# Units 4 and 5 computed by halves of a chunk, and one visit of block 1 placed eight matmuls later

## The chip, the cores and the metric

The kernel runs on one core of a Trainium2 chip. The core has five engines with a queue of instructions each: PE (TensorE, matmuls, with PEld for its weight loads), DVE (VectorE), ACT (ScalarE), POOL (GpSimd) and SP (SyncE, which here only issues DMAs). The metric is the time of one execution on the device in microseconds (us).

## The reference

Two layers follow each other. The first is retention, a recurrence with a 64x64 state for each of 8 heads and 4 batches over 768 tokens. The second is a feed-forward network over all 3072 tokens with a parametric ReLU:

```python
for t in range(S):
    state = gamma * state + outer(k[:, :, t], v[:, :, t])
    y[:, :, t] = scale * (q[:, :, t] @ state)
x = y.transpose(0, 2, 1, 3).reshape(B * S, H * D)   # 3072 x 512
h = x @ w_in                                        # 512 x 2048
g = maximum(h, 0) + alpha * minimum(h, 0)
out = g @ w_out                                     # 2048 x 512
```

## The kernel before, in words

**Tiling.** Tokens are taken in 12 units of 256, three to a batch. A unit has two chunks of 128 tokens (`c` = 0, 1), and a chunk has two halves of 64 (`r` = 0, 1). The 8 heads are four pairs (`p`), with `a` the head within a pair. Two units are a block of 512 tokens; there are six blocks.

**Retention of a unit.** Instead of token by token it goes by chunks: products k·v summed over tokens (tiles `st`), a running state (`tf`, the state after the decay; `th`, its copies in 16 bits for the matmuls), scores k·q within the chunk (`sca`, `scb`), scores times a causal mask (`m`), and the output `y`, which is the state times q plus the masked scores times v. `y` is copied to `xT`, the input of the feed-forward network.

There are two forms of this in the kernel.

- *By chunks* (`sum_mm`, `state_sum`, `score_mm`, `masks`, `out_mm`): one state per chunk; the scores of the first half of the tokens run against all 128 queries of the chunk and those of the second half against 64.
- *By halves* (`halves_mm`, `middle`, `behind_middle`, `middle_copy`, `half_mm`, `half_masks`, `halves_out`): the sums stay apart for each half, a second state `tm` stands in the middle of the chunk, and scores are needed only within a half. `tm` is copied to 16 bits into one of six buffers `tgbuf`: the near half of the partitions by POOL, the far half by ACT (`part=1`). For each chunk, DVE makes `tm`, then `ss`; POOL multiplies `ss` by the decay and gives `tf`, from which DVE makes the next chunk's `tm`.

In the kernel before, units 4 and 5 go by chunks, and units 6 to 11 by halves (`MID = 6`).

**The loop around it.** The order of all work on every engine is written out by hand; no scheduler moves anything, and each engine takes its instructions in the order in which the code issues them. In pass `n` of the last loop (n = 1 to 4) the second layer of block n is computed and the retention of block n+1 is put between its matmuls. "Block 1" is the pass n = 1, with `u0` = 4 and `u1` = 5.

The second layer (`ffn2_seven`) is seven products of 16 matmuls each, called p1 to p7 below in their order, with a yield behind each matmul; `tick(gen, m)` issues m of them. They accumulate in two PSUM banks, `ox` (bank 0) and `oy` (bank 1):

- p1 writes `ox`; ACT copies `ox` to `oy` (`moves`).
- p2 adds to `ox`; ACT copies `ox` out as `os` (`kept`).
- p3 adds to `oy`; ACT copies `oy` out as `cu`.
- p4 begins `ox` anew.
- p5 adds to `oy`; ACT copies `oy` out as a second `cu`, which DVE adds to `ox` (`plus`).
- p6 adds to `oy` again; ACT copies it out as `ot`.
- p7 adds to `ox`; DVE adds the first `cu` and gives `os`.

A product that writes a bank waits until the copy out of that bank is done. In the code this stands as:

```python
        yield from product(oy, gs(1), ws(1), False)
        u2 = kept(oy)
        yield
        ox = bank(x, "ox")
        yield from product(ox, gs(0), ws(0), True)
        yield
        yield from product(oy, gs(2), ws(2), False)
        u3 = kept(oy)
        plus(ox, u3, "o1")
        yield
        yield from product(oy, gq(1, 1), ws(3), False)
```

**The visits.** Three times in a pass the retention's matmuls are put between those of the products. The *first visit*, behind p1 (`tick(gen, 16)`), has the sums of both units and the scores of `u0`. The *second*, in the middle of p4 (after ticks of 8, 9, 15 and 8), has the output of `u0` and the scores of `u1`. The *third*, behind p5 in all passes before (`tick(gen, 24)`), has the output of `u1`; four matmuls of the next block's first layer follow it (`begin(n + 1)`), then the rest of the products.

**Queries.** `move_q` copies the queries into a second arrangement `qf`. In block 1, ACT does it, in two instructions for each unit; for later units it is a DMA.

**Sums for p3 to p7.** `g_sums` are DVE additions over the whole activated tile. In block 1, DVE does the first two of them in one piece each, 2048 elements per partition, right before it turns to the retention; in later blocks they are in pieces of 1024, of which the first pieces come earlier.

Of the kernel before, what the change touches and what calls it, by code (L numbers as in the profile page):

```python
# [22 lines left out]
def kernel(  # L23
# [21 lines left out]


    SPLIT = 4
    MID = 6
    U = 256
    UPB = S // U  # L50
    NU = B * UPB
# [42 lines left out]
    HF, HM = NFT // 2, d_model // 2  # L94
# [16 lines left out]
    tgbuf = [tgall[:, i] for i in range(6)]  # L111
# [137 lines left out]
    def sum_mm(u, banks, half=0):  # L249

        kdq, _, vx = prepped[u]
        last = u % UPB == UPB - 1
        cs = (0,) if last else (0, 1)
        if half == 0:
            sums["t"] = [ps(banks[0], "st0"), ps(banks[1], "st1")]
        for p in range(NP):
            for r in range(2):
                for c in cs:
                    for a in range(2):
                        nc.tensor.matmul(  # L260
                            out=sums["t"][c][rows(a), 256 * half + 64 * p : 256 * half + 64 * p + 64],
                            lhsT=kdq[rows(c), 0, r, 2 * p + a, :],
                            rhs=vx[rows(c), 2 * p + a, r, :],
                            start=(r == 0),
                            stop=(r == 1),
                        )
        for c in cs:
            sums[u, c] = sums["t"][c][:, 256 * half : 256 * half + 256].rearrange(
                "p (a e) -> p a e", e=64
            )  # L270
# [23 lines left out]
    def middle(u, c):  # L294

        s = sums.pop((u, c))
        m = sbp.tile([128, NP, 64], FP, tag="tm", bufs=2, name=f"tm{u}_{c}")
        if u % UPB == 0 and c == 0:
            nc.vector.tensor_copy(out=m, in_=s[:, 0])
        else:  # L300
            nc.vector.tensor_tensor(out=m, in0=run.pop(), in1=s[:, 0], op=ADD)  # L301
        middle_copy((u, c, m), 0)
        return u, c, m, s
# [13 lines left out]
    def middle_copy(uct, part):  # L317

        u, c, t = uct[:3]
        if u not in mids:  # L320

            mids[u] = tgbuf[u - MID].rearrange("p n i -> p (n i)").rearrange(
                "p (a n e) -> p a n e", a=2, n=NP
            )
        for a in range(2):
            if (a != c) != part:
                continue
            if part:
                nc.scalar.activation(
                    out=mids[u][rows(c), a], in_=t[rows(a)], func=COPY, bias=0.0, scale=1.0  # L330
                )
            else:
                nc.gpsimd.tensor_copy(out=mids[u][rows(c), a], in_=t[rows(a)])  # L333
# [20 lines left out]
    def half_masks(u, a):  # L354
        m2 = sbp.tile([128, 512], F16, tag=f"m2{a}{u % 2}", bufs=2, name=f"m2{a}")
        nc.vector.tensor_tensor(
            out=m2.rearrange("p (x i) -> p x i", x=8),
            in0=live[u][a].rearrange("p (x i) -> p x i", x=8),
            in1=mj[:, 256:320].unsqueeze(1).to_broadcast([128, 8, 64]),
            op=MULT,  # L360
        )
        live[u][a] = m2
# [51 lines left out]
    def state_sum(u, c, eng):  # L414
        if (u, c) not in sums:
            return None
        s = sums.pop((u, c))
        t = sbp.tile([128, NP, 64], FP, tag="tf", bufs=3, name=f"tf{u}_{c}")
        if u % UPB == 0 and c == 0:
            nc.vector.tensor_tensor(out=t, in0=s, in1=dec, op=MULT)  # L420
        else:
            ss = sbp.tile([128, NP, 64], FP, tag="ss", bufs=2, name=f"ss{u}_{c}")
            nc.vector.tensor_tensor(out=ss, in0=run.pop(), in1=s, op=ADD)  # L423
            eng.tensor_tensor(out=t, in0=ss, in1=dec, op=MULT)  # L424
        run[:] = [t]
        return u, c, t
# [532 lines left out]
    def tick(gen, m=10**6):  # L959
        for _ in range(m):  # L960
            if next(gen, 1) == 1:
                return
# [225 lines left out]
    for n in range(1, NBLK):  # L1188
        more = n + 1 < NBLK
        u0 = 2 * (n + 1)  # L1190
        if n > 1:
            gen = begun
            if more:
                for u in (u0, u0 + 1):
                    i = rescale(G, u, 0, 0, 8)
                    if u == u0:
                        behind(i, gate)
                    rescale(G, u, 1, 0, 8)
                    turn_dma(u)
                    cast_v(G, u)  # L1200
                    if u > u0:
                        load(u + 1, "qv")
                    else:
                        load(u + 2, "k")
                    move_q(u)
                    tick(gen, 8)
            tick(gen)
            if not more:
                for i in (2, 4):
                    for lo in (0, 4):  # L1210
                        g_sums(n, i, lo, lo + 4)
                g_sums(n, 0, 0, HF)
                g_sums(n, 3, 0, HF)
        gen = ffn2_seven(n, 0, 1) if more else ffn2_seven(n, 0, 1, (2, 3, (4, 6)))
        if more and u0 >= MID:
            u1 = u0 + 1
            tick(gen, 16)
            halves_mm(u0, (2, 3))
            halves_mm(u1, (6, 7))
            half_mm(u0, (4, 5))  # L1220
            m00 = middle(u0, 0)
            s00 = behind_middle(m00)
            half_masks(u0, 0)
            state_copy(s00, part=0)
            m01 = middle(u0, 1)
            s01 = behind_middle(m01)
            state_copy(s01, part=0)
            tick(gen, 8)
            middle_copy(m00, 1)
            state_copy(s00, part=1)  # L1230
            middle_copy(m01, 1)
            tick(gen, 9)
            half_masks(u0, 1)
            m10 = middle(u1, 0)
            s10 = behind_middle(m10)
            state_copy(s10, part=0)
            load(u0 + 3)
            g_sums(n, 2, 0, HF)
            tick(gen, 15)
            state_copy(s01, part=1)  # L1240
            middle_copy(m10, 1)
            tick(gen, 8)
            halves_out(u0, (2, 3))
            half_mm(u1, (4, 5))
            half_masks(u1, 0)
            state_copy(s10, part=1)
            m11 = middle(u1, 1)
            middle_copy(m11, 1)
            half_masks(u1, 1)
            s11 = behind_middle(m11)  # L1250
            state_copy(s11, part=0)
            gate = g_sums(n, 3, 0, HF)
            tick(gen, 24)
            halves_out(u1, (4, 5), evict=False)
            begun = begin(n + 1)
            take_y(u1, (0, 1))
            state_copy(s11, part=1)
            if n == NBLK - 2:
                in_sums(6, 0, V)
                in_sums(6, 1, V)  # L1260
                x_sums(n + 1, V)
                in_sums(4, 0, V)
                in_sums(4, 1, V)
        elif more:
            tick(gen, 16)
            sum_mm(u0, (2, 3))
            sum_mm(u0 + 1, (2, 3), half=1)
            score_mm(u0, 0, (4, 5))
            score_mm(u0, 1, (6, 7))
            s00 = state_sum(u0, 0, G)  # L1270
            state_copy(s00, part=0)
            masks(u0, 0)
            s01 = state_sum(u0, 1, G)
            tick(gen, 8)
            move_q(u0, A)
            state_copy(s00, part=1)
            state_copy(s01, part=0)
            tick(gen, 9)
            masks(u0, 1)
            move_q(u0 + 1, A)  # L1280
            s10 = state_sum(u0 + 1, 0, G)
            state_copy(s10, part=0)
            load(u0 + 3)
            s11 = state_sum(u0 + 1, 1, G)
            state_copy(s11, part=0)
            g_sums(n, 2, 0, HF)
            tick(gen, 15)
            state_copy(s01, part=1)
            state_copy(s10, part=1)
            tick(gen, 8)  # L1290
            out_mm(u0, (4, 5))
            score_mm(u0 + 1, 0, (6, 7))
            score_mm(u0 + 1, 1, (2, 3))
            state_copy(s11, part=1)
            masks(u0 + 1, 0)
            masks(u0 + 1, 1)
            gate = g_sums(n, 3, 0, HF)
            tick(gen, 24)
            out_mm(u0 + 1, (4, 5), evict=False)
            begun = begin(n + 1)  # L1300
            take_y(u0 + 1, (0, 1))
        tick(gen)
        if n == NBLK - 2:
            in_sums(6, 2, V)
            in_sums(6, 3, V)
            in_sums(4, 2, V)
            in_sums(4, 3, V)
# [30 lines left out]
```

## Time and profile before

| what | value |
|---|---|
| median of 3 runs | 198.33 us (198.26 to 198.95) |
| profiled execution | 198.86 us, of which the span from the first to the last instruction is 196.9 us |
| PE busy | 189.3 us (96%) |
| DVE, ACT, POOL busy | 156.3 (79%), 115.4 (59%), 106.1 us (54%) |
| granted clock of TensorE | 0.997 on average |
| pass n = 1, from p1 to the first layer of block 2 | 66.44 to 82.13 us |
| pass n = 4, from p1 to the mixed first layer | from 153.37 us on |

The span is the stretch that the trace sees; the profiled execution's own time is 2.0 us longer. Times in the trace count from the span's start. Pass n = 4 matters for reading: its units 10 and 11 are the second and third of their batch, as units 4 and 5 are, and they go by halves already.

### The profile page before, as it was taken

The numbers are of one execution on the slowest core, as the hardware profiler recorded it, in microseconds if no ns is written. First come the engines' busy times: TensorE is split into PE (matmuls) and PEld (weight loads), VectorE is DVE, ScalarE is ACT, GpSimd is POOL, SyncE is SP. The second block draws the span as 40 slices with busy tenths as digits, with TensorE's granted clock in tenths as the row PEclk, the third lists the DMA queues.
The fourth block names the chain that finished last, engine by engine and source line by source line (L and its number), as shares of the span: only waits on it lengthen the run. The fifth ranks groups of instructions, "written<-read, shape, count | busy, mean of one in ns | idle before, by whom it ended". The sixth has DMA issues, their size and how long they took to land.

```text
span 196.9 us, 6085 instructions
## 1 busy us (share of the span) xinstructions
PE 189.3 (96%) x2529; PEld 128.8 (65%) x2529; DVE 156.3 (79%) x259; ACT 115.4 (59%) x199; POOL 106.1 (54%) x113
## 2 busy tenths in 40 slices
PE   6688999999999999999999999999999999999993
PEld 2356645568467688744688744788644788865882
DVE  7698987517698998289988389977489996999983
ACT  4458665349187668467467476467466486678110
POOL 3176897499549544970077980076970180039300
PEclk9999999999999999999999999999999999999998
DMA  5999999998879989898988899929865010400014
GB/s 156 313 317 380 374 381 377 293 180 136 211 192 200 286 197 265 213 311 175 213 203 209 256 201 191 222 65 225 256 122 126 17 57 3 160 3 0 0 65 152
DMA packets 90026, 37.92 MB, mean 193 GB/s; under 512 B 57984, under 2 KB 87696, under 8 KB 90000
## 3 DMA queue, kind: packets, MB, share of 16 engines
q1 hardware_dynamic: 88768, 36.45, 69.2%
q0 software_dynamic: 1056, 1.05, 3.6%
q8 instruction: 20, 0.33, 0.6%
q10 hardware_dynamic: 176, 0.04, 0.1%
q14 instruction: 6, 0.05, 0.1%
HBM read 27.31 MB, written 6.29 MB: 171 GB/s over the span
## 4 chain that ended last, share of the span: by engine, by line
PE 90%; SPq 4%; DMA 3%; DVE 0%; issue 0%; POOL 0%; DVEq 0%
PE hps L632 36%; PE ox L857 16%; PE oy L857 12%; PE ops L809 7%; SPq L165 4%; PE hps L719 4%; PE sp L761 3%; DMA vs<-in_v_dram 3%; PE y L533 1%; PE y L384 1%; PE trb L230 1%; PE st L284 1%; PE sca L466 1%; PE ov L857 1%; PE ow L857 1%; PE oz L857 1%
## 5 line engine op out<-in xcount | busy, mean ns | idle before, releaser
L632 PE MATMUL hps<-xT,win 128*128 128x512 f16 (+1 forms) x396 | 71.5, 338 | 0.3 <-DVE ss L423 0.3
L650 DVE SCALAR_TENSOR_TENSOR gt<-hm,oma,hps 128x512 f16<-128x512 f32 (+1 forms) x96 | 59.4, 656 | 12.1 <-issue 4.3
L648 ACT ACTIVATE hm<-hps 128x512 f32<-128x512 f32 x80 | 47.6, 597 | 24.6 <-PE hps L632 22.5
L632 PEld LDWEIGHTS <-win 128*128 128x128 f16 x396 | 38.1, 98 | 31.0 <-POOL win L978 0.4
L857 PEld LDWEIGHTS <-gs 128*128 128x128 f16 x320 | 31.0, 98 | 3.7
L857 PEld LDWEIGHTS <-gt 128*128 128x128 f16 x240 | 22.9, 98 | 4.0
L333 POOL CAST tg<-tm 64x256 f16<-64x256 f32 x12 | 4.8, 396 | 34.3 <-DVE tm L301 22.3
L185 POOL TENSOR_TENSOR kdq<-qs,tab 128x1024 f16<-128x1024 f32 (+1 forms) x12 | 20.2, 1686 | 3.0 <-DVE wsum L572 2.3
L185 POOL TENSOR_TENSOR kdq<-ks,tab 128x1024 f16<-128x1024 f32 (+1 forms) x12 | 20.2, 1686 | 2.6 <-PE y L515 2.6
L857 PE MATMUL ox<-wout,gt 128*128 128x256 f16 x144 | 17.3, 273 | 0.0
L857 PE MATMUL oy<-wsum,gs 128*128 128x256 f16 x144 | 17.2, 273 | 0.0
L556 ACT ACTIVATE xT<-y 128x512 f16<-128x512 f32 x22 | 14.9, 744 | 3.1 <-PE y L533 2.0
L201 POOL CAST vx<-vs 128x1024 f16<-128x1024 f32 (+1 forms) x13 | 12.6, 970 | 6.7 <-DMA vs<-in_v_dram 6.7
L809 PE MATMUL ops<-wout,gt 128*128 128x512 f16 x64 | 15.3, 380 | 0.0
L613 DVE TENSOR_TENSOR gs<-gt 128x1024 f16<-128x1024 f16 (+1 forms) x14 | 13.0, 934 | 0.2
L877 ACT ACTIVATE cu<-oy 128x512 f32<-128x512 f32 x10 | 6.0, 597 | 10.6 <-PE oy L857 10.1
L236 ACT ACTIVATE kq<-trb 128x1024 f16<-128x1024 f16 x8 | 8.2, 1023 | 6.3 <-PE trb L230 6.3
L313 POOL TENSOR_TENSOR tf<-ss,tab 128x256 f32<-128x256 f32 x10 | 10.3, 1028 | 2.5 <-DVE ss L312 1.3
L881 DVE TENSOR_TENSOR os<-ox,cu 128x512 f32<-128x512 f32 x5 | 3.4, 687 | 10.1 <-PE ox L857 10.1
L670 POOL TENSOR_SCALAR hn<-qc,oma 128x256 f32<-128x256 f32 x4 | 4.5, 1138 | 12.4 <-DVE qc L785 12.3
L809 PEld LDWEIGHTS <-gt 128*128 128x128 f16 x64 | 5.8, 98 | 6.0
L424 POOL TENSOR_TENSOR tf<-ss,tab 128x256 f32<-128x256 f32 x6 | 5.9, 980 | 7.1 <-DVE ss L423 7.1
(119 smaller groups left out, 293.1 us busy)
## 6 DMA issues: line engine op xcount, KB each, us to landing
qs<-in_q_dram SPq DMA_DIRECT2D x9, 512.0 KB, 5.4
ks<-in_k_dram SPq DMA_DIRECT2D x32, 128.0 KB, 3.5
vs<-in_v_dram SPq DMA_DIRECT2D x32, 128.0 KB, 4.6
early<-in_moe_w_in_dram SPq DMA_DIRECT2D x7, 512.0 KB, 7.5
out_dram<-os SPq DMA_DIRECT2D x9, 256.0 KB, 2.5
early<-in_moe_w_out_dram SPq DMA_DIRECT2D x4, 512.0 KB, 7.0
out_dram<-ot SPq DMA_DIRECT2D x4, 512.0 KB, 3.8
ks<-in_k_dram SPq DMA_DIRECT2D x6, 256.0 KB, 6.1
```

The lines of the kernel that those rows point to most:

```text
L165: nc.sync.dma_start(out=t[nm[0]][:, h, :], in_=src[b, h, U * c : U * c + U, :].rearrange("h (p r) d -> p h (r d)", r=2),)
L185: return eng.tensor_tensor(out=kdq[:, t, :, h0:h1, :].rearrange("p r h d -> p h r d"), in0=staged[u]["kq"[t]][:, h0:h1, :].rearrange("p h ...
L201: eng.tensor_copy(out=o, in_=i)
L236: nc.scalar.activation(out=kq.rearrange("p (x a) i -> p x a i", x=4)[:, :, 2 * hh : 2 * hh + 2, :], in_=trb.rearrange("p (x a i) -> p x a ...
L313: nc.gpsimd.tensor_tensor(out=t, in0=ss, in1=dec, op=MULT)
L556: nc.scalar.activation(out=o, in_=i, func=COPY, bias=0.0, scale=1.0,)
L613: last_g.append(nc.vector.tensor_tensor(out=o, in0=a, in1=b, op=op))
L632: nc.tensor.matmul(out=hps[:, f, U * (ul - lo) : U * (uh - lo)].rearrange("p (u t) -> p u t", t=U), lhsT=w_in_all[:, hp, 128 * (f0 + f) : ...
L648: nc.scalar.activation(out=hm, in_=hps, func=RELU, bias=0.0, scale=-1.0)
L650: nc.vector.scalar_tensor_tensor(out=gt[:, f0 + f, U * lo : U * hi], in0=hm[:, f, :], scalar=oma_sb[:, f0 + f : f0 + f + 1], in1=hps[:, f, :],
L809: nc.tensor.matmul(out=opss[tq], lhsT=gt[:, ft, 128 * tq : 128 * tq + 128], rhs=w_out_all[:, ft, :], start=(ft == 0), stop=(ft == NFT - 1),)
L857: nc.tensor.matmul(out=o[1][m], lhsT=lhs(f, m), rhs=rhs(f), start=(first and f == 0 and (m == 0 or o[0] is None)), stop=(f == HF - 1), ski ...
```

## The change

`MID` goes away, so units 4 and 5 take the same path by halves as units 6 to 11. The buffers `tgbuf` are counted from unit 4 on, modulo six, instead of from unit 6. Block 1 keeps its `move_q` on ACT, now inside the common path, and its third visit comes after 32 ticks instead of 24, which is behind the first eight matmuls of p6 instead of behind p5. The branch that held the work by chunks is deleted.

```diff
-    MID = 6
...
-            mids[u] = tgbuf[u - MID].rearrange("p n i -> p (n i)").rearrange(
+            mids[u] = tgbuf[(u - SPLIT) % len(tgbuf)].rearrange("p n i -> p (n i)").rearrange(
...
-        if more and u0 >= MID:
+        if more:
             u1 = u0 + 1
             tick(gen, 16)
             halves_mm(u0, (2, 3))
...
             s01 = behind_middle(m01)
             state_copy(s01, part=0)
             tick(gen, 8)
+            if n == 1:
+                move_q(u0, A)
             middle_copy(m00, 1)
             state_copy(s00, part=1)
             middle_copy(m01, 1)
             tick(gen, 9)
             half_masks(u0, 1)
+            if n == 1:
+                move_q(u1, A)
             m10 = middle(u1, 0)
...
             gate = g_sums(n, 3, 0, HF)
-            tick(gen, 24)
+            tick(gen, 24 if n > 1 else 32)
             halves_out(u1, (4, 5), evict=False)
             begun = begin(n + 1)
...
-        elif more:
-            tick(gen, 16)
-            sum_mm(u0, (2, 3))
-            sum_mm(u0 + 1, (2, 3), half=1)
-            score_mm(u0, 0, (4, 5))
-            score_mm(u0, 1, (6, 7))
-            s00 = state_sum(u0, 0, G)
-            state_copy(s00, part=0)
...
-            move_q(u0, A)
-            state_copy(s00, part=1)
-            state_copy(s01, part=0)
-            tick(gen, 9)
...
-            gate = g_sums(n, 3, 0, HF)
-            tick(gen, 24)
-            out_mm(u0 + 1, (4, 5), evict=False)
-            begun = begin(n + 1)
-            take_y(u0 + 1, (0, 1))
```

One line of the program is gone, so a line L877 of the kernel before is L876 in the changed one.

On ACT, the piece of block 1 from the copy of `ox` to `oy` on to the first `cu` (`oy`, `os` and `cu` are the copies named above; `qf` are moved queries; `th` and `tg` are 16-bit copies of the states `tf` and `tm`). Before:

```order
L877 ACTIVATE oy<-ox 128x512
L218 ACTIVATE qf_1394<-kq_1021 64x512 x2
L450 ACTIVATE th_1132<-tf_0_1373 64x256
L877 ACTIVATE os<-ox 128x512
L218 ACTIVATE qf_1416<-kq_1063 64x512 x2
L877 ACTIVATE cu<-oy 128x512
```

With the change:

```order
L876 ACTIVATE oy<-ox 128x512
L217 ACTIVATE qf_1408<-kq_1021 64x512 x2
L328 ACTIVATE tg<-tm_0_1381 64x256
L449 ACTIVATE th_1132<-tf_0_1385 64x256
L328 ACTIVATE tg<-tm_1_1391 64x256
L876 ACTIVATE os<-ox 128x512
L217 ACTIVATE qf_1428<-kq_1063 64x512 x2
L876 ACTIVATE cu<-oy 128x512
```

The copy `os` now stands behind two copies of middle states, the second of them of chunk 1.

On DVE, the same stretch of block 1, from the last `g_sums` in one piece on (`m` are masked scores, `ss` and `tm` the states). Before:

```order
L613 TENSOR_TENSOR gs_1265<-gs_1265,gt_861 128x2048
L423 TENSOR_TENSOR ss_0_1374<-tf_1_1054,st_1287 128x256
L479 TENSOR_TENSOR m_1378<-sca,mi 128x384
L479 TENSOR_TENSOR m_1380<-scb,mi 128x384
L423 TENSOR_TENSOR ss_1_1383<-tf_0_1373,st_1288 128x256
```

With the change:

```order
L612 TENSOR_TENSOR gs_1265<-gs_1265,gt_861 128x2048
L300 TENSOR_TENSOR tm_0_1381<-tf_1_1054,st_1287 128x256
L311 TENSOR_TENSOR ss_0_1384<-tm_0_1381,st_1287 128x256
L355 TENSOR_TENSOR m_1388<-sca,mi 128x512
L300 TENSOR_TENSOR tm_1_1391<-tf_0_1385,st_1288 128x256
```

The state of chunk 1 in the middle (`tm_1`) is DVE's fourth instruction behind the sums, and it needs POOL's `tf_0`.

On PE, the end of p5 and what follows it in block 1, with the engines waited for (`gs` belongs to p5, `gt` to p6; `y` is the third visit, `hps` the next block's first layer). Before:

```order
L857 MATMUL oy<-wsum,gs_1265 128x256
L515 LDWEIGHTS th_1398 [waits Pool_49]
L515 MATMUL y_1591<-kq_1063,th_1398 64x128 [waits Activation_49]
...
L632 MATMUL hps<-xT_1515,win 128x256 [waits PE_49]
...
L857 LDWEIGHTS gt_861
L857 MATMUL oy<-wsum,gt_861 128x256 [waits Activation_49]
```

With the change:

```order
L856 MATMUL oy<-wsum,gs_1265 128x256
L856 LDWEIGHTS gt_861
L856 MATMUL oy<-wsum,gt_861 128x256 [waits Activation_49]
...
L383 LDWEIGHTS th_1398 [waits Pool_49]
L383 MATMUL y_1629<-kq_1063,th_1398 64x2x32 [waits DVE_49]
```

The first matmul of p6, which waits for ACT's copy of `oy`, stood behind the visit and four matmuls of `hps`, and now stands right behind the last matmul of p5.

More of the change, by code (lines that the diff above doesn't have):

```diff
@@ L1263 @@
                 in_sums(4, 1, V)
-        elif more:
-            tick(gen, 16)
-            sum_mm(u0, (2, 3))
-            sum_mm(u0 + 1, (2, 3), half=1)
-            score_mm(u0, 0, (4, 5))
-            score_mm(u0, 1, (6, 7))
-            s00 = state_sum(u0, 0, G)
-            state_copy(s00, part=0)
-            masks(u0, 0)
-            s01 = state_sum(u0, 1, G)
-            tick(gen, 8)
-            move_q(u0, A)
-            state_copy(s00, part=1)
-            state_copy(s01, part=0)
-            tick(gen, 9)
[L1279 to L1296, printed above, removed]
-            gate = g_sums(n, 3, 0, HF)
-            tick(gen, 24)
-            out_mm(u0 + 1, (4, 5), evict=False)
-            begun = begin(n + 1)
-            take_y(u0 + 1, (0, 1))
         tick(gen)
```

## The prediction

> **What bounds the kernel now.** I read first who waits for whom on PE (columns: wait in all, times, longest), then the chain of waits in pass n = 1 and pass n = 4 (start, length, what), and last the timelines of ACT and DVE beside them.
>
> ```profile
> PE 189.3 (96%) x2529; PEld 128.8 (65%) x2529; DVE 156.3 (79%) x259; ACT 115.4 (59%) x199; POOL 106.1 (54%) x113
> ...
> PE kps L106 <- DVE spin L1004: 1.5, 1, 1.5
> ...
> PE st L260 <- POOL vx L201: 0.2, 1, 0.2
> ```
>
> These are the first and the last of the six waits that PE has; they add up to 4.0 us and none is in pass 1 or later. Block 1 is one gapless row of matmuls on PE:
>
> ```profile
> 68.19 0.56 PE st L260 x44
> ...
> 69.16 1.85 PE ox L857 x16
> 71.01 1.75 PE oy L857 x16
> 72.76 0.87 PE ox L857 x8
> 73.63 0.35 PE y L515 x16
> ...
> 74.68 0.98 PE ox L857 x8
> 75.66 1.75 PE oy L857 x16
> 77.40 0.35 PE y L515 x16
> ...
> 78.10 0.54 PE hps L632 x4
> 78.64 1.75 PE oy L857 x16
> ```
>
> The three visits are 68.19 to 69.16 (0.97), 73.63 to 74.68 (1.05) and 77.40 to 78.10 (0.70); p2 to p6 are the rows of L857. So PE sets the end: a matmul less is a gain, and any wait that PE gets here is a loss in full, since behind it PE has no wait that could swallow it. Pass 4 does by halves what block 1 will do:
>
> ```profile
> 155.15 0.56 PE st L284 x49
> ...
> 156.02 1.85 PE ox L857 x16
> 157.87 1.75 PE oy L857 x16
> 159.62 0.87 PE ox L857 x8
> 160.49 0.38 PE y L384 x32
> ...
> 161.43 0.98 PE ox L857 x8
> 162.41 1.75 PE oy L857 x16
> 164.15 0.39 PE y L384 x32
> ...
> 164.80 0.54 PE sp L761 x4
> ```
>
> **PE's own work: −0.26 us.** The change adds 40 matmuls (8 sums, since both halves stand apart; 16 in each output, since each half has its own state) and makes many of the others half as long. Rather than count, I take pass 4's visits, whose units have the same place in their batch: 0.87, 0.94 and 0.65 against 0.97, 1.05 and 0.70. That is −0.10, −0.11 and −0.05. This price is nearly exact. [...]
>
> **First wait: p4 behind `os`.** p4 begins bank 0 anew and must wait until ACT has copied p2's result (`os`). ACT now has two copies of middle states ahead of that copy. The second needs DVE's chunk-1 state, which needs POOL's product, which needs DVE's chunk-0 state. How late that chain starts is DVE's matter: in block 1 it first finishes a sum of 2048 elements in one piece, in pass 4 a piece of 1024 (DVE of both passes):
>
> ```profile
> 69.15 1.23 DVE L613 TENSOR_TENSOR gs<-gs,gt 128x2048 f16<-128x2048 f16 x1
> 70.29 0.41 DVE L423 TENSOR_TENSOR ss<-tf,st 128x256 f32<-128x256 f32 x1
> ...
> 156.15 0.41 DVE L301 TENSOR_TENSOR tm<-tf,st 128x256 f32<-128x256 f32 x1
> ```
>
> From the first visit's start to DVE's first retention instruction it is 70.29 − 68.19 = 2.10 us in block 1 and 156.15 − 155.15 = 1.00 us in pass 4. The chain is the same from there, so it comes out 1.10 us later against PE. ACT in pass 4:
>
> ```profile
> 158.27 0.41 ACT L329 ACTIVATE tg<-tm 64x256 f16<-64x256 f32 x1
> 158.71 0.60 ACT L877 ACTIVATE os<-ox 128x512 f32<-128x512 f32 x1
> ...
> 160.34 0.41 ACT L450 ACTIVATE th<-tf 64x256 f16<-64x256 f32 x1
> 160.66 0.40 ACT L329 ACTIVATE tg<-tm 64x256 f16<-64x256 f32 x1
> 161.18 1.35 ACT L556 ACTIVATE xT<-y 128x512 f16<-128x512 f32 x2
> ```
>
> There `os` is done at 159.31, 4.16 us behind the first visit's start, and p4 starts at 159.62 (4.47), so 0.31 us are to spare. In block 1 `os` will be done at 68.19 + 4.16 + 1.10 = 73.45, and PE wants p4 at 68.19 + 4.47 = 72.66. In the kernel before, `os` had only one state copy ahead and made it:
>
> ```profile
> 68.72 1.25 ACT L218 ACTIVATE qf<-kq 64x512 f16<-64x512 f16 x2
> 71.50 0.41 ACT L450 ACTIVATE th<-tf 64x256 f16<-64x256 f32 x1 [1.53 <-POOL tf L424]
> 71.94 0.60 ACT L877 ACTIVATE os<-ox 128x512 f32<-128x512 f32 x1
> 72.56 1.27 ACT L218 ACTIVATE qf<-kq 64x512 f16<-64x512 f16 x2
> 73.85 0.60 ACT L877 ACTIVATE cu<-oy 128x512 f32<-128x512 f32 x1
> ...
> 77.44 0.60 ACT L877 ACTIVATE cu<-oy 128x512 f32<-128x512 f32 x1 [0.74 <-PE oy L857]
> ```
>
> (72.54 against 72.76.) The step from ACT's end to PE I read where PE waited for ACT:
>
> ```profile
> 36.24 1.02 ACT L236 ACTIVATE kq<-trb 128x1024 f16<-128x1024 f16 x1 [1.17 <-PE trb L230]
> ...
> 37.32 0.26 PEld L466 LDWEIGHTS <-kq 64*64 64x64 f16 x16 [0.53 <-ACT kq L236]
> ```
>
> 37.32 − 37.26 = 0.06 us. So the first wait is 73.45 + 0.06 − 72.66 = **0.85 us**. It would be 0 if the chain started as early as in pass 4; at the top I allow 1.2, should the chain be late by one more state copy of 0.4. I take 0.85, since each link's length is seen in pass 4, and 0.3 to either side of it inside this case. `move_q` of unit 4, issued at 68.72 and done at 69.97, is over before the first state is there, so it costs nothing; without that cover its 1.25 us would fall on `os`.
>
> **What that wait hides.** With p4 at 73.51, p5 comes at 73.51 + 2.79 (pass 4's 162.41 − 159.62) = 76.30. The sum that p5 needs comes from the same chain on DVE and is late by the same 1.10 against PE; behind the wait of 0.85 only 0.25 of that is left, and PE did not wait there in pass 4.
>
> **Second wait: p6 behind `cu`.** p6 adds to bank 1, which ACT must first copy out (`cu`, 0.60) when p5 is done. Before, the third visit and the four matmuls of the next block covered that: 78.64 − 77.40 = 1.24 us. With 32 ticks, p6 follows p5 with nothing between. With ACT idle that is 0.04 (77.40 to 77.44) + 0.60 + 0.06 = 0.70 us. ACT is not idle: `os` ends at 73.45, `qf` of unit 5 takes 1.27, the first `cu` 0.60, then two state copies, `xT` 1.35, two state copies again, with 0.02 between; a pair of state copies takes 0.75, as they overlap (160.34 to 161.06 in pass 4). That is 73.45 + 1.29 + 0.62 + 0.75 + 1.37 + 0.75 = 78.23, while p5 ends at 76.30 + 1.75 = 78.05. So `cu` runs 78.24 to 78.84, p6 starts at 78.90, and the second wait is **0.85 us** (bounds 0.70 and 1.1). Queued behind this `cu` are the two `xT` of unit 5; 28 matmuls lie between the third visit and their use, 3.1 us at 0.11 each against 1.35 for the copies, so nothing follows. The later visit also avoids a small wait: ACT's last state copy ends at 78.23, 0.2 us after p5, and the output of unit 5 needs it.
>
> **The rest at nothing.** DVE's four masks of 512 replace eight of 384 in the same stretch, beside the matmuls; one that came late would add its lateness to the visit that uses it. POOL's four more copies stand ahead of block 2's rescaling, before which POOL was idle for 2.57 us; SP's order is the same, and what it stores is ready before its turn.
>
> ```profile
> 77.87 1.90 POOL L185 TENSOR_TENSOR kdq<-ks,tab 128x1024 f16<-128x1024 f32 x1 [2.57 <-PE y L515]
> ```
>
> Without that cover the rescaling would come later by the copies' length, some 0.4 each as on ACT, and PE uses it only in block 2's first visit, behind a whole first layer.
>
> **Sum.** −0.26 + 0.85 + 0.85 = +1.44 us. Against the profiled execution, 198.86 + 1.44 = 200.30; that execution is 0.53 above the median of the runs, so I forecast 198.33 + 1.44 = **199.8 us**, 0.7% slower.
>
> **Rivals.**
>
> - *Only p6 waits.* If `os` comes in time, ACT is earlier too and the second wait is 0.70: −0.26 + 0.70 = +0.44, 198.8 us. For it speaks that pass 4 has 0.31 to spare; against it DVE's 2.10.
> - *Not slower: both waits stay under cover.* This needs `os` by 72.66, so that p4 is on time, and `cu` done when p6's turn comes; then only −0.26 remains, 198.1 us. The place that decides is p6's first matmul: were it held by the first `cu` alone, which is done by 75.4, nothing would stand there. Against it: in the order p6 is directly behind p5, both write bank 1, and the copy of p5's result reads it in between for 0.60.
> - *More than two waits.* POOL's product in the chain runs beside DVE's work, or the granted clock falls after the waits. A product of 1.75 us at half the clock would cost another 1.75: 201.5 us. Against it: PE's waits at 35 to 38 us left the clock as it was. [...]
>
> ```profile
> 35.60:38.00 2.40, 2.37 (x50) 1.48 (x47) 1.29 (x2) 1.02 (x1) 0.84 (x1) 1.00 1.00 290
> ```
>
> (The column behind POOL's is the granted clock, 1.00.)
>
> [...]
>
> **How the numbers follow.** Both waits 0.67 (199.3 to 200.4 from the bounds −0.26 + 0.55 + 0.70 and −0.26 + 1.2 + 1.1); only p6 0.14; neither 0.10; more 0.07; dear matmuls 0.02. The range 198.5 to 200.6 holds the first two and a part of "more". About 0.5% (1.0 us) is what a measurement here can tell from no change. Slower by more: nearly all of the first, "more" and the last, less the low edge: 0.72. Within: only p6 and most of "neither", 0.25. Faster: the tail of "neither", 0.03, as the work saved is 0.13%.
>
> **What would show it.** In the changed profile PE should wait for ACT's `os` in front of p4 (0.8 to 0.9) and for `cu` in front of p6 (0.7 to 1.0), two waits that the list of before lacks, and the three visits should take 0.87, 0.94 and 0.65. From the first visit's start to p6's end it should take 13.6 us instead of 68.19 to 78.64 + 1.75, which is 12.2, and all passes behind it keep their length. I am wrong if `os` ends more than 0.1 us before p3 does, if p6 starts on p5's heels, or if a later pass gives the time back.

## The result, and the profile after

The changed kernel takes 200.1 us (median of 11 runs) where the kernel before takes 198.43 us; the ratio is 1.0069 with a 95% interval of 1.0047 to 1.0091. (The ratio is formed from all the runs; the quotient of the two medians is 1.0084.) By the interval the change costs 0.9 to 1.8 us. The forecast was 199.8 us, 0.7% slower. The span of the profiled execution went from 196.9 to 198.9 us.

The list of what PE waits for, in the changed kernel (wait in all, times, longest), has two entries that it did not have:

```profile
PE ox L856 <- ACT os L876: 0.8, 1, 0.8
PE oy L856 <- ACT cu L876: 0.7, 1, 0.7
```

PE's timeline in block 1, its large matmuls alone (in brackets the idle time before and who ended it):

```profile
66.40 1.91 PE L856 MATMUL ox<-wout,gt 128*128 128x256 f16 x16
...
73.61 1.03 PE L856 MATMUL ox<-wsum,gs 128*128 128x256 f16 x8 [0.82 <-ACT os L876]
...
79.05 1.03 PE L856 MATMUL oy<-wsum,gt 128*128 128x256 f16 x8 [0.68 <-ACT cu L876]
```

The two rows with a bracket are the first halves of p4 and p6. ACT at the same time:

```profile
70.86 0.41 ACT L328 ACTIVATE tg<-tm 64x256 f16<-64x256 f32 x1 [0.77 <-DVE tm L300]
72.07 0.41 ACT L449 ACTIVATE th<-tf 64x256 f16<-64x256 f32 x1 [0.80 <-POOL tf L312]
72.53 0.41 ACT L328 ACTIVATE tg<-tm 64x256 f16<-64x256 f32 x1
72.97 0.60 ACT L876 ACTIVATE os<-ox 128x512 f32<-128x512 f32 x1
...
77.79 0.40 ACT L328 ACTIVATE tg<-tm 64x256 f16<-64x256 f32 x1
78.40 0.60 ACT L876 ACTIVATE cu<-oy 128x512 f32<-128x512 f32 x1 [0.21 <-PE oy L856]
```

`os` stands behind three state copies, and ahead of each of the first two ACT sat idle for some 0.8 us, until DVE and then POOL had made the state; `os` ends at 73.57, and p4 starts at 73.61. The second `cu` starts when p5 is done, ends at 79.00, and p6 starts at 79.05. The chain of waits of the changed kernel goes through both copies (start, length, what):

```profile
72.98 0.59 ACT os L876
73.57 0.04 issue
73.61 1.03 PE ox L856 x8
...
78.40 0.61 ACT cu L876
79.01 0.04 issue
79.05 1.03 PE oy L856 x8
...
83.91 13.39 PE hps L631 x64
```

To compare kernels I use one length throughout: from the start of ACT's copy of p1 (`oy`) to the first matmul of the next block's whole first layer on PE. It was 68.22 to 82.13, 13.91 us, before; it is 68.34 (ACT) to 83.91 in the changed kernel, 15.57 us. That is 1.66 us more, and the medians differ by 1.67. The two ends before, from ACT's timeline and from the chain:

```profile
68.22 0.58 ACT L877 ACTIVATE oy<-ox 128x512 f32<-128x512 f32 x1 [1.15 <-PE ox L857]
```

```profile
82.13 0.87 PE hps L632 x6
```

### The profile page after: what moved, and what is told of

It is laid out like the page before. It is cut to its first block, busy times and chain, and to the rows that moved or that the text cites. A ratio compares the mean times of both kernels' runs of the same rounds, so it can differ in the third digit from the quotient of the medians.

```text
span 198.9 us, 6175 instructions
## 1 busy us (share of the span) xinstructions
PE 190.5 (96%) x2569; PEld 129.4 (65%) x2569; DVE 156.7 (79%) x259; ACT 116.7 (59%) x203; POOL 107.6 (54%) x117
## 4 chain that ended last, share of the span: by engine, by line
PE 82%; DMA 5%; SPq 5%; ACT 3%; DVE 2%; issue 1%; POOL 1%; ACTq 0%; DVEq 0%
PE hps L631 28%; PE ox L856 15%; PE oy L856 12%; PE ops L808 7%; PE hps L718 3%; DMA early<-in_moe_w_out_dram 3%; PE sp L760 3%; PE kps L105 2%; PE trb L229 2%; DMA ks<-in_k_dram 1%; PE y L383 1%; SPq L987 1%; SPq L164 1%; PE y L397 1%; SPq L204 1%; PE sca L465 1%
## 5 line engine op out<-in xcount | busy, mean ns | idle before, releaser
L332 POOL CAST tg<-tm 64x256 f16<-64x256 f32 x16 | 6.3, 396 | 39.8 <-DVE tm L300 27.2
L312 POOL TENSOR_TENSOR tf<-ss,tab 128x256 f32<-128x256 f32 x13 | 13.0, 998 | 2.9 <-DVE ss L311 1.3
L876 ACT ACTIVATE cu<-oy 128x512 f32<-128x512 f32 x10 | 6.0, 597 | 10.2 <-PE oy L856 9.6
L977 POOL CAST win<-early 128x1024 f16<-128x1024 f32 (+1 forms) x8 | 7.5, 931 | 3.5 <-DMA early<-in_moe_w_in_dram 3.4
```

The costliest lines, as they stand in the source:

```text
L312: nc.gpsimd.tensor_tensor(out=t, in0=ss, in1=dec, op=MULT)
L977: return eng.tensor_copy(out=o, in_=i)
```

## The experiments

The theory: all of the loss is two waits of PE in block 1, p4's for `os` (late because three state copies stand ahead of it and DVE starts their chain late) and p6's for `cu` (because the visit that covered that copy is now behind p6's first half). The rivals: the later visit was needed and saves as much as it costs; the waits hang together, so that one grows when the other goes; the work by halves costs time of its own in block 1.

| kernel | time, us | ratio to before, 95% interval | length in block 1, us |
|---|---|---|---|
| before | 198.43 | 1 | 13.91 |
| the change | 200.1 | 1.0069 (1.0047 to 1.0091) | 15.57 |
| e1: third visit behind p5 | 199.37 | 1.0043 (1.0011 to 1.0076) | 14.70 |
| e2: `os` first | 199.52 | 1.0041 (1.0018 to 1.0064) | 14.97 |
| e3: both | 199.03 | 1.0011 (0.9989 to 1.0032) | 14.13 |
| e4: before, third visit later | 199.58 | 1.0047 (1.0021 to 1.0073) | 14.75 |
| e5: e3, p5's sum first | 198.93 | 1.0007 (0.9984 to 1.0030) | 14.00 |
| e6: `os` behind two copies | 199.9 | 1.0062 (1.0037 to 1.0086) | 15.36 |
| e7: half of two sums left out | 199.61 | 1.0044 (1.0023 to 1.0065) | 14.78 |
| e8: e5, next layer's four matmuls first | 198.66 | 0.9998 (0.9972 to 1.0025) | 13.82 |

The ratios are against runs of the kernel before on the same chip, whose median there was 198.6 to 198.7. The lengths come from one profiled execution each. By the intervals, the change, e1, e2, e4, e6 and e7 are slower than before, and e3, e5 and e8 can't be told from it; how the versions differ among themselves is read from the lengths and the waits.

**e1: the third visit back behind p5.**

```diff
-            tick(gen, 24 if n > 1 else 32)
+            tick(gen, 24)
```

> The changed kernel with the third visit of block 1 back behind p5 (24 ticks). Theory of two waits: the wait of p6 for the copy of p5's result goes (0.7 us and the slow restart behind it, p6's first eight matmuls 1.03 instead of 0.87), since visit and four matmuls cover 0.60 of copying with 1.2 us; the wait of p4 for os stays at 0.8. About 199.2 us, 0.4% above before. Rival, that the later visit was needed: unit 5's output then waits for ACT's last state copy (done 0.2 us before p5's end in the changed kernel's trace, so I expect no wait); with such a wait of 0.7 the time stays at 200.1.

Measured: 199.37 us, ratio 1.0043; the length falls by 0.87 to 14.70. In the list of PE's waits the second of the two is gone and the first stands:

```profile
PE ox L856 <- ACT os L876: 0.8, 1, 0.8
...
PE y L500 <- ACT tg L449: 0.2, 1, 0.2
```

The last row belongs to unit 3, long before; there is no entry for unit 5's output. In ACT's timeline the last state copy runs 76.95 to 77.35, p5 ends by 77.50 and `cu` starts at 77.54:

```profile
76.95 0.40 ACT L328 ACTIVATE tg<-tm 64x256 f16<-64x256 f32 x1
77.54 0.60 ACT L876 ACTIVATE cu<-oy 128x512 f32<-128x512 f32 x1 [0.19 <-PE oy L856]
```

So the later visit avoided nothing here. The rival falls.

**e2: `os` first on ACT.**

```diff
             if n == 1:
                 move_q(u0, A)
+                tick(gen, 9)
             middle_copy(m00, 1)
             state_copy(s00, part=1)
             middle_copy(m01, 1)
-            tick(gen, 9)
+            if n > 1:
+                tick(gen, 9)
```

> The changed kernel with ACT's copy of p2's result (os) ahead of the three state copies of unit 4; PE's order is the same. Theory: the wait of p4 goes (0.8 us and 0.16 for the restart). But ACT's work behind it is not less: PE reaches p5's end 1 us earlier and ACT does not, so the wait of p6 grows from 0.7 to about 1.0. About 199.4 us, 0.45% above before, with one wait. Rival, that the two waits have nothing to do with each other: the wait of p6 stays 0.7 and the time falls by the whole 0.95, to 199.15. Rival, that os is not what p4 waits for: no change, 200.1.

Measured: 199.52 us, ratio 1.0041; the length falls by 0.60 to 14.97. p4 no longer waits; p6 waits 0.7 as before. The time is the expected one, but the reason is not: the wait of p6 did not grow. Instead p5 now starts late, because of the sum that DVE makes for it (DVE's row, then the chain's):

```profile
74.70 1.22 DVE L612 TENSOR_TENSOR gs<-gt 128x2048 f16<-128x2048 f16 x1
```

```profile
74.79 1.15 DVE gs L612
75.93 0.05 issue
75.98 1.93 PE oy L856 x16
```

The sum ends at 75.92 and p5 follows at 75.98; its 16 matmuls take 1.93 in the chain instead of 1.75. This lateness was there all along, behind the wait of p4.

**e3: both edits.** `os` first as in e2 and `tick(gen, 24)` as in e1.

> Both edits at once: os first and the third visit behind p5. Theory: neither of the two waits is left; p5 ends about 0.3 us before ACT's last state copy for unit 5 is done, so the third visit waits some 0.35 with a restart of 0.16 behind it. The work saved is 0.26. About 198.7 us, 0.1% above before. Rival, that units 4 and 5 by halves cost time of their own on PE or DVE whatever the waits: 199.2 or more.

Measured: 199.03 us, ratio 1.0011 with an interval on both sides of 1; the length is 14.13, 0.22 above before. So the two waits together are nearly the whole loss. What is left is not the third visit's wait, as I had expected, but p5's for DVE's sum. From the list of what the weight loads wait for:

```profile
PEld L856 <- DVE gs L612: 0.4, 1, 0.4
```

**e4: the kernel before, with the third visit alone moved.**

```diff
             gate = g_sums(n, 3, 0, HF)
-            tick(gen, 24)
+            tick(gen, 32)
             out_mm(u0 + 1, (4, 5), evict=False)
```

> The kernel before with only the third visit of block 1 moved eight matmuls later (32 ticks). Theory: p6 then follows p5 with nothing between and waits for ACT's copy of p5's result, 0.04 + 0.60 + 0.06 = 0.70 us, with 0.16 for the restart: about 199.3 us, 0.4% above before. Rival, that the move alone is harmless and the second wait comes from ACT's longer queue: 198.4, within 0.1%.

Measured: 199.58 us, ratio 1.0047; the length rises by 0.84 to 14.75. Units 4 and 5 go by chunks here, and the wait is the same as in the changed kernel:

```profile
79.59 1.03 PE L857 MATMUL oy<-wsum,gt 128*128 128x256 f16 x8 [0.69 <-ACT cu L877]
```

The move of the visit costs this much by itself, with ACT's queue as it was before. The two parts of the change nearly add up: work by halves alone (e1) lengthens block 1 by 0.79, the visit alone by 0.84, both together by 1.66.

**e6: `os` between the state copies.** The changed kernel, with `os` behind two of the three copies.

```diff
             middle_copy(m00, 1)
             state_copy(s00, part=1)
+            if n == 1:
+                tick(gen, 9)
             middle_copy(m01, 1)
-            tick(gen, 9)
+            if n > 1:
+                tick(gen, 9)
```

> The changed kernel (third visit late, as it is there) with os behind the first two of unit 4's three state copies, ahead of the third. Theory: os starts with POOL's first decayed state copied, 0.45 us earlier than in the changed kernel, so p4 waits 0.35 instead of 0.8 and p6's wait stays 0.7: about 0.45 us, 0.2%, below the changed kernel, 0.45% above before. Rival, that p4 waits for something else on ACT: still 0.8.

Measured: 199.9 us, ratio 1.0062; the length falls by only 0.21 to 15.36. Both of PE's waits moved:

```profile
72.91 1.03 PE L856 MATMUL ox<-wsum,gs 128*128 128x256 f16 x8 [0.28 <-ACT os L876]
...
78.59 1.03 PE L856 MATMUL oy<-wsum,gt 128*128 128x256 f16 x8 [0.96 <-ACT cu L876]
```

The first went from 0.82 to 0.28: `os` moved by 0.45, and PE's first visit happened to take 0.08 longer in this profile. The second grew from 0.68 to 0.96, which I had expected to stay. ACT shows why: PE comes sooner, and ACT is not done with its queue when p5 ends, so `cu` follows the last state copy without idle time.

```profile
77.52 0.40 ACT L328 ACTIVATE tg<-tm 64x256 f16<-64x256 f32 x1
77.94 0.60 ACT L876 ACTIVATE cu<-oy 128x512 f32<-128x512 f32 x1
```

This is the coupling that I had put into e2's expectation. In e2 DVE's late sum hid it, since it made p5 late too.

**e7: DVE starts its chain earlier.** The changed kernel, in which DVE makes only half of the two sums ahead of the retention in block 1. The other half is left out, and POOL fills its place with zeros, so this kernel serves for its time alone.

```diff
                 hi = HF if f0 == NFT - 1 else 4
+                if n == 1:
+                    hi = 4
+                    gsums[n] = sbp.tile([128, 4, HF, U], F16, tag="gt", bufs=2, name=f"gs{n}")
+                    nc.gpsimd.memset(gsums[n][:, 0:2, 4:8, :], 0.0)
```

> The changed kernel, but DVE makes only the first half (1024 of 2048 elements) of the two sums ahead of the retention in block 1; the other half is left out and filled with zeros by POOL in its idle time. ACT's and PE's order are the changed kernel's. Theory: DVE starts its chain 1.0 us earlier, about where it starts in pass 4, so os is done in time and p4 does not wait (at most 0.1); p6 still waits 0.7: about 0.9 us below the changed kernel, 0.3% above before. Rival, that ACT's queue is too long by itself, whenever DVE starts (moved queries of 1.25 and three copies ahead of os): p4 still waits 0.5 to 0.8.

Measured: 199.61 us, ratio 1.0044; the length falls by 0.79 to 14.78. ACT's order is that of the changed kernel, and still `os` is in time: DVE's first state starts 0.91 us behind p1's end (68.69 against 67.78) instead of 2.10 (70.41 against 68.31), the first of ACT's idle times is gone, the second is down from 0.80 to 0.35, and the one wait of block 1 is p6's 0.7. DVE's first state in the changed kernel, then here:

```profile
70.41 0.41 DVE L300 TENSOR_TENSOR tm<-tf,st 128x256 f32<-128x256 f32 x1
```

```profile
68.69 0.41 DVE L300 TENSOR_TENSOR tm<-tf,st 128x256 f32<-128x256 f32 x1
```

```profile
70.36 0.42 ACT L449 ACTIVATE th<-tf 64x256 f16<-64x256 f32 x1 [0.35 <-POOL tf L312]
70.81 0.41 ACT L328 ACTIVATE tg<-tm 64x256 f16<-64x256 f32 x1
71.25 0.60 ACT L880 ACTIVATE os<-ox 128x512 f32<-128x512 f32 x1
```

```profile
72.23 1.04 PE L860 MATMUL ox<-wsum,gs 128*128 128x256 f16 x8
...
77.74 1.03 PE L860 MATMUL oy<-wsum,gt 128*128 128x256 f16 x8 [0.69 <-ACT cu L880]
```

So it takes both for the first wait: the copies ahead of `os`, and DVE's late start. With either taken away it is gone.

**e5: p5's sum first.** On top of e3, DVE makes the sum for p5 ahead of unit 5's first state.

```diff
+            if n == 1:
+                g_sums(n, 2, 0, HF)
             m10 = middle(u1, 0)
             s10 = behind_middle(m10)
             state_copy(s10, part=0)
             load(u0 + 3)
-            g_sums(n, 2, 0, HF)
+            if n > 1:
+                g_sums(n, 2, 0, HF)
```

> os first and the third visit behind p5, and besides DVE makes the sum that p5 needs ahead of unit 5's first state instead of behind it. In the kernel without this last edit PE's one wait in block 1 was p5's, for that sum (0.27 us and 0.17 of restart). Theory: it goes, no wait of PE is left in block 1, and what remains of the change is the work saved, 0.26 us: from p1's end to the next first layer 13.7 us instead of 13.94, and a time of 0.1% below before. Rival: POOL's decay product runs beside the sum and takes 1.46 instead of 0.61, so unit 5's states come late and the third visit waits by 0.2 to 0.4: no gain against before, 0.1% above it.

Measured: 198.93 us, ratio 1.0007; the length is 14.00, not 13.7. p5 is on time, and now the third visit waits. Its state matmuls take 0.65 in the chain, against 0.37 to 0.38 elsewhere:

```profile
75.45 1.75 PE oy L856 x16
77.19 0.65 PE y L383 x32
```

The visit's first loads are in time, at 77.12, and p5 ends at 77.19. Then it halts twice:

```profile
76.56 0.68 DVE L355 TENSOR_TENSOR m<-scb,mi 128x512 f16<-128x512 f32 x1
```

```profile
76.98 0.40 ACT L328 ACTIVATE tg<-tm 64x256 f16<-64x256 f32 x1
```

```profile
77.30 0.21 PE L383 MATMUL y<-kq,th 64*64 64x64 f16 x1
...
77.44 0.21 PE L383 MATMUL y<-kq,tg 64*64 64x64 f16 x1
```

The first halt ends 0.06 behind DVE's second mask (76.56 + 0.68 = 77.24), which reads unit 5's scores in a bank that the visit writes; the second ends 0.06 behind ACT's last state copy (76.98 + 0.40 = 77.38). These causes are read from the times, since the list of waits puts the idle time of the weight loads here down to a copy of POOL, which was done by 77.10. POOL's product took 0.61, so the rival's outcome came by another way: the sum now stands ahead of unit 5's states on DVE, which makes the mask late, and ACT's queue, which carries 1.27 us of moved queries of unit 5 in this stretch, was next in line.

**e8: the next layer's four matmuls first.** On top of e5.

```diff
-            halves_out(u1, (4, 5), evict=False)
-            begun = begin(n + 1)
+            if n == 1:
+                begun = begin(n + 1)
+            halves_out(u1, (4, 5), evict=False)
+            if n > 1:
+                begun = begin(n + 1)
```

> The kernel with os first, the third visit behind p5 and p5's sum first, and besides the four matmuls of block 2's first layer ahead of the third visit instead of behind it (their input is ready by then). In the kernel without this last edit PE's weight loads for the third visit waited some 0.3 us for ACT's last copy of a state. Theory: the four matmuls (0.54) cover that, p6 has the visit alone (0.65) as cover for the copy of 0.60, and block 1 has no wait: from ACT's copy of p1 to the next first layer 13.65 us (before: 13.91; without this edit: 14.00), and a time of 198.2, 0.1% below before, which the runs can just not tell from no change. Rival: the copy in front of p6 is no longer covered whole and p6 waits 0.1 to 0.2: 13.8 to 13.9, no gain against before.

Measured: 198.66 us, ratio 0.9998 (0.9972 to 1.0025); the length is 13.82. PE has no wait left in block 1:

```profile
75.16 1.75 PE oy L856 x16
76.90 0.44 PE hps L631 x4
77.34 0.38 PE y L383 x32
77.72 0.29 PE y L397 x32
78.01 1.85 PE oy L856 x16
```

With no wait anywhere, the work by halves is 0.09 us shorter than before, not the 0.26 that I had forecast. A gain of that size is far below what the runs can tell; within their interval the version is as fast as the kernel before, and no version was found that is faster than the kernel before.

## Why the prediction was right, and which terms were off

**The first wait: right, cause and place.** I had `os` done 5.26 us behind p1's end (73.45 − 68.19); it was 73.57 − 68.31 = 5.26. e2 removes it by the order on ACT, e7 by DVE's start, and e6 sets it in between.

**The second wait: right in cause, its size by another path.** I had ACT still busy when p5 ends, by 0.2 us. In the changed kernel, counted from p1's end, p5 ended 0.19 later than I had it (mostly the missing term below) and ACT's last state copy 0.16 sooner; ACT was idle for 0.21, and the wait is the bare copy: 0.68, just under my lower bound of 0.70. e4 gives the same 0.69 with another ACT queue. Where PE is earlier, as in e6, ACT's queue does decide, with 0.96.

**A term that was missing: what PE loses beside the listed idle time.** I took the times of the chain of waits as the starts of matmuls. In the timeline, p4's first matmul started at 72.59 in the kernel before while p3 ended at 72.76, since by the ends that the trace models one matmul starts before the last is done:

```profile
70.85 1.91 PE L857 MATMUL oy<-wsum,gs 128*128 128x256 f16 x16
72.59 1.04 PE L857 MATMUL ox<-wsum,gs 128*128 128x256 f16 x8
```

After a wait that overlap of 0.17 is lost. It shows in the chain as 1.03 for eight matmuls instead of 0.87, twice, 0.32 us in all.

**PE's own work: the size was off.** −0.26 came from pass 4. With visits read as the gap between the large matmuls around them (modelled end to next start, so a little shorter than in the chain), the ten profiles give: by chunks in block 1 (before, e4) 0.90, 0.97 to 0.98 and 0.63; by halves in block 1, where no wait falls into them, 0.82 to 0.95, 0.89 to 1.01 and 0.60; in pass 4, 0.80 to 0.81, 0.86 to 0.87 and 0.57 to 0.58. So in block 1 the first two visits scatter by 0.12 to 0.13, and only in pass 4 are they always as short as I took them for. In the changed kernel the gain was 0.08 + 0.05 + 0.03 = 0.16.

**The sum** by these terms: idle 0.82 + 0.68, lost overlap 0.32, work −0.16, together 1.66, as in the profile. The forecast 0.85 + 0.85 − 0.26 = 1.44 had the waits too long by 0.20, the work saved too large by 0.10, and lacked the 0.32. That these errors partly cancel is luck. With an interval of 0.9 to 1.8 us the runs can't tell 1.44 from 1.66; that the terms were off is known from the profiles alone.

**What the first wait hides:** right. I had written that the sum for p5 is late by the same cause and that the wait of p4 swallows it; with that wait gone, e2 and e3 show PE at that sum.

**The later visit:** I gave it a small use, 0.2 us, on the ground that ACT's last state copy would end after p5. With p4 waiting it ends before p5 does (e1); only when both DVE and ACT's order are mended (e5) does the third visit meet that copy, and DVE's second mask before it.

**The rivals.** "Only p6 waits" is what e2 and e7 made by force, at 199.5 and 199.6. That is more than the 198.8 that I had put on it: its sum lacked the lost overlap too, took the work saved at 0.26, and in e2 p5 is late besides. "Both waits stay under cover" falls by the two rows of waits. The 0.02 that the forecast gives to dear matmuls rested on a price for each of the forty more matmuls, which no run shows: e8, with all of them and no wait, is not longer than the kernel before (13.82 against 13.91 us), and the 32 matmuls `y L383` of a visit take 0.37 to 0.38 us in the chain where nothing holds them, 12 ns each. The granted clock stayed at 1.00 in both waits:

```profile
69.24:72.84 3.60, 3.56 (x32) 3.04 (x31) 3.31 (x6) 1.98 (x5) 1.59 (x4) 1.00 0.80 180
72.84:73.61 0.77, 0.00 (x0) 0.00 (x0) 0.71 (x2) 0.72 (x3) 0.69 (x2) 1.00 0.66 150
...
78.38:79.05 0.67, 0.00 (x1) 0.00 (x0) 0.22 (x2) 0.60 (x1) 0.33 (x1) 1.00 1.05 298
```

(The stretch before the first wait, the first wait, and the second; behind the stretch's length stands PE's busy time, and the clock is the third number from the end.) In these two kernels' traces a lower clock stands only behind PE's last matmul. Before, that matmul ends at 193.65, and the clock is 1.00 up to 195.6 and 0.50 from 195.8 to the end; in the changed kernel it ends at 195.72, and the clock is 1.00 up to 197.8 and 0.50 from 198.0. The two waits, 0.82 and 0.68 us, are both shorter than the 1.9 us or more of idleness at 1.00 there; what a longer wait in block 1 would do to the clock is not shown. The row that the prediction cites for the clock, 35.60 to 38.00, says little of it: PE was busy there for 2.37 of 2.40 us, and only its weight loads waited.

**The later passes kept their length** but for scatter: pass 2's first two visits were 0.1 us longer in the profile of the changed kernel, and in e2, whose block 1 is late as well, they were not. These 0.2 us, and 0.1 us ahead of block 1, nearly account for what the span's 2.0 has beyond the 1.66 of block 1.

## What to carry to other kernels

Where an engine takes its instructions in order, a copy out of an accumulator belongs ahead of whatever waits for another engine (with `os` ahead of the three state copies, in e2, p4's wait of 0.82 us was gone). Before moving work, list what each accumulation waits for and what covers that copy, since the work that is moved away can be the cover, as the third visit was here (p6 waited 0.69 us in e4). A wait can hide the next one: after each repair read the list again, for here `os`, DVE's sum and ACT's last copy stood one behind the other, and a stretch where several engines are nearly full (73.61 to 78.38 in the changed kernel, 4.77 us, has DVE busy for 4.53 and ACT for 4.49) gave back part of what a repair gained (e2, e6, e5). A price taken from another stage of the same kernel may not hold: the first visit by halves took 0.80 to 0.81 us in pass 4 and up to 0.95 in block 1.

## What the runs showed of the hardware

The short matmuls of the visits scatter where the large ones do not: 16 matmuls of a product right behind another product took 1.75 to 1.76 us in the chain where nothing held them, while the first visit of block 1 by halves took 0.82 to 0.95 us in eight kernels. In pass 4 the same visit took 0.80 to 0.81 in all ten profiles. The windows of the kernel before and of the changed kernel show the largest difference between the two places in the share of the DMA engines, the last column but one (these are pass 4's first visit before, and block 1's first visit after; the windows reach some 0.06 and 0.11 us into p2):

```profile
155.15:156.02 0.87, 0.87 (x89) 0.83 (x90) 0.84 (x2) 0.58 (x1) 0.00 (x0) 1.00 0.00 0
```

```profile
68.31:69.24 0.93, 0.93 (x89) 0.89 (x90) 0.93 (x1) 0.90 (x2) 0.00 (x0) 1.00 1.18 280
```

By the gap between the large matmuls these two visits took 0.81 and 0.82, so most of the difference between the two rows lies behind the visit. ACT is busier in block 1 too (0.90 us against 0.58). In pass 3, where ACT has 0.58 as in pass 4 and transfers run (a share of 0.81 before and 0.85 in the changed kernel), the same visit took 0.84 to 0.97, so ACT alone does not explain it. That the transfers slow the visit is a guess from this, and a weak one: in the changed kernel the visit took 0.82 in block 1 at a share of 1.18, and 0.84 in pass 3 at 0.85. No run here took the transfers away at that place, and the cause stays open.
